# The token gate's dot product on VectorE, V in whole tiles, and a new order, in a hand-planned attention and feed-forward kernel

## The chip, the core and the metric

The kernel runs on one core of one Trainium2 chip. A core has five engines that run side by side: TensorE (PE, matrix products), VectorE (DVE), ScalarE (ACT), GpSimd (POOL) and SyncE (SP), which here only issues DMAs. Each engine takes its instructions strictly in the order in which the program lists them, and one that waits for a semaphore holds up all behind it. The metric is device time in microseconds (us), a median over runs.

## The reference

Two branches read the same `x` (2048 rows of 512, bf16) and are mixed by a gate for each row:

```python
x = A_x
g = _sigmoid((x * gate_w).sum(-1, keepdims=True))
a = _A_ref(x, A_wq, A_wk, A_wv, A_wo, A_beta)
b = _B_ref(x, B_W_gate, B_W_up, B_W_down)
return g * a + (1 - g) * b
```

`_B_ref` is a feed-forward block with 1792 hidden columns: `gate = x @ W_gate`, `up = x @ W_up`, `h = relu(gate) * up`, `h @ W_down`. `_A_ref` is attention with 32 heads of 16 columns in four segments of 512 rows. For each segment `s`:

```python
logits = einsum('bhqd,bhkd->bhqk', qs, ks) * scale + mask
a_dot = einsum('bhqk,bhkd->bhqd', softmax(logits), vs)
a_mem = einsum('bhld,bhde->bhle', phi(qs), M) / den
o = g * a_mem + (1.0 - g) * a_dot            # g = sigmoid(beta), per head
M = M + einsum('bhld,bhle->bhde', phi(ks), vs)   # likewise z, for den
```

with `phi(t) = t + 1 where t > 0, else exp(t)`; then `o @ wo`. The gate of a row is thus a dot product of that row of `x` with `gate_w`, and it is this dot product that the change moves.

## The kernel before

Every piece of work is a step of a planner. `add(name, engines, emit, after, prio, lat, take, give)` gives a step its possible engines with a cost on each, the steps it waits for, a due number (`prio`), the time `lat` until its result counts as there, and the PSUM banks that it takes or gives back. `lay_out` plays the plan through by these costs: whenever an engine comes free it takes, of the steps whose predecessors are done, the one with the lowest rank. The rank is `prio`, plus the entry of `SHIFT` for the step's kind, plus a tenth of the step's own entry in `NUDGE`, a list of 1090 numbers in the order in which steps are added. An engine that is free takes any step that is ready, however late its rank. The order that results is written out as the program. On the chip only the order stays, with semaphores; the costs and due times are the plan's alone.

PSUM holds four banks `rb` of 512 columns for all products but the attention scores, which have four banks of their own (`sp`).

The steps that matter here, by segment `seg`, column block `c` and row tile `t` of 128 rows:

- **Start.** `early` steps are DMAs issued at once on SP or ACT: the four row tiles of segment 0 (into `xn`, the same memory as `xT[1]`), then V's, K's and Q's weights. `E_G` stands for the load of `gate_w` and `beta` into `gin` by POOL, and counts as landed at 6.0. `XP` steps transpose the row tiles on PE, `XA` steps copy them to `xT[0]` on DVE or ACT. `YP`, `YD`, `YA`, `YH`, `YL` compute the heads' gates; `YP` also turns `gate_w` into a column, which `YD` copies into column 512 of `wv_sb`.
- **Weights of the feed-forward.** `wg0`..`wg3` and `wu0`..`wu3` are eight DMAs on SP, `wd` and `wo` the down and output weights. `wd` waits for the transposes of K's features in segment 0.
- **Projections.** `Q`, `K` (L491) and their copies `QC`, `KC`; `KO` masks K (L504, L506). V of segment 0 (L516) comes piece by piece as its weight lands. V of the later segments (L533) is done in two halves of 256 columns for each row tile, the second with column 512, the token gate, behind it: 257. `VC` copies a half (L389, L387), and the second half's also clamps the gate's column into `zg` (L543). For segment 0 `TP` (L579) is a product of its own for the column, `TG` (L587) its clamp.
- **Row gates.** `TE` (L593) takes the exponential of `zg`, `TN` (L598) and `TL` (L603, L606) go on from it.
- **Attention.** `QK` (L738) fills `sp`, `EX` (L749) is its exponential on ACT, `MK` (L759) the mask on POOL, `PV` (L808) the product with V, followed by a chain on DVE.
- **Memory.** `EK` (L626) takes the exponential of K into `e1k`, `MN` (L632) its minimum with 1, `PK` (L636) puts phi(K) into `pkT`, and `KX` is a DMA transpose of `pkT` into `pK`, issued on SP. `XT` steps are DMA transposes of segments 1 to 3 of `x`.
- **Feed-forward.** `G`, `U` (L918), `R` (L930, L932), `H` (L937), `D` (L952), `W` (L965), `OS`, and the store `ST` on SP.

Of the kernel before, what the change touches and what calls it, by code (L numbers as in the profile page):

```python
# [13 lines left out]
P = 128  # L14
# [24 lines left out]
SHIFT = {'PA': 15, 'PB': 0, 'LIKE': 35, 'T': -43, 'PQ': 42, 'N': -104, 'MZ': -228, 'PV': -136, 'OS': -150, 'OC': -94, 'R': -63, 'EX': -241, 'QK': -81, 'KC': 5, 'H': -95, 'KTR': -235, 'TG': -121, 'PK': -281, 'VC': -64, 'MN': 30, 'XC': 118, 'MK': 208, 'K': -25, 'U': 10, 'D': 11, 'EK': 57, 'MQ': 24, 'EQ': -42, 'TR': 201, 'MA': -36, 'KO': 124, 'V': -15, 'G': 8, 'QC': 201, 'KX': 50, 'W': 72, 'Q': -21, 'OX': 45, 'TA': -65, 'GS': 41, 'TL': -45, 'TN': 103, 'TB': 8, 'MR': 0}  # L39
# [181 lines left out]
def mm(n, k=1):  # L221
    return k * (n / 2400.0 + 0.0025)
# [806 lines left out]
```

## Time and profile before

| | |
|---|---|
| median of 3 runs | 269.93 us (269.28 to 272.64) |
| the profiled execution, its time | 270.74 us |
| its span in the profile | 269.0 us |
| clock granted to PE | 1.0 |
| DMA, read and written | 8.13 and 2.10 MB of device memory |

The page of the profile gives busy time and count of instructions of each engine, the chain of work that ended last, and the costliest groups. A timeline lists start and duration in us, the engine, the line in the kernel, the operation, `out<-in` with shapes, and a count; a bracket gives the idle time of the engine just before and what released it. PEld is PE's weight load, SPq the DMA queue of SP. Windows give busy us of each engine within stretches of the span:

```
0.00:5.00 5.00, 3.67 (x29) 2.98 (x30) 1.17 (x10) 2.23 (x4) 4.13 (x12) 1.00 0.58 166
5.00:10.00 5.00, 4.99 (x27) 2.17 (x25) 1.36 (x7) 2.77 (x7) 3.27 (x8) 1.00 0.94 291
10.00:16.00 6.00, 6.00 (x50) 2.78 (x48) 3.77 (x10) 4.30 (x8) 3.28 (x8) 1.00 1.09 369
16.00:24.00 8.00, 8.00 (x66) 3.33 (x66) 5.04 (x11) 7.03 (x6) 2.70 (x6) 1.00 1.09 260
24.00:36.00 12.00, 10.52 (x125) 5.20 (x131) 9.10 (x23) 10.10 (x13) 7.67 (x16) 1.00 0.93 150
36.00:80.00 44.00, 43.94 (x754) 20.30 (x751) 36.16 (x82) 37.46 (x35) 31.47 (x80) 1.00 0.24 59
80.00:130.00 50.00, 50.00 (x746) 22.26 (x745) 39.14 (x89) 39.90 (x36) 32.75 (x72) 1.00 0.12 29
```

The columns after the stretch and its length are PE, PEld, DVE, ACT and POOL with their instruction counts, the granted clock, the busy share of the DMA engines, and GB/s.

### The profile page before, as it was taken

To read this page: it belongs to the slowest core of one execution; us is meant where nothing else is said; L and a number is where in the kernel's file an instruction comes from. 1 tells how busy PE (TensorE), PEld (TensorE's weight loads), DVE (VectorE), ACT (ScalarE), POOL (GpSimd) and SP (SyncE) were. 2 spreads that over 40 slices of the span, in tenths; PEclk is the share of its full clock that TensorE was granted. 3 is DMA by queue.
4 is the path that set the end of the run, shared out by engine and by line. 5 is a ranking of instruction groups with operands and counts; after the bars stand their busy time and mean duration, and the time that the engine had idled before them with its cause. 6 is when DMAs were issued, how large, how long until landed. Compare 5 with 4: busy or idle time off the path is not lost.

```text
span 269.0 us, 8042 instructions
## 1 busy us (share of the span) xinstructions
PE 263.0 (98%) x3365; PEld 120.9 (45%) x3365; DVE 185.3 (69%) x414; ACT 192.3 (71%) x185; POOL 162.4 (60%) x378
## 2 busy tenths in 40 slices
PE   8999799999999999999999999999999999999995
PEld 5444344444455444444444544444444444344444
DVE  1477697799489966986767767897826535878800
ACT  3789799987689977777979777765659757876021
POOL 8435767465888874655684888645425685735400
PEclk9999999999999999999999999999999999999999
DMA  6997980420302310000030000000010100000011
GB/s 202 327 347 150 120 273 5 57 66 2 80 2 73 73 43 22 2 2 0 13 68 22 23 19 2 23 4 0 2 45 22 37 5 22 0 4 2 2 39 39
DMA packets 26293, 15.06 MB, mean 56 GB/s; under 512 B 13585, under 2 KB 26257, under 8 KB 26257
## 3 DMA queue, kind: packets, MB, share of 16 engines
q1 hardware_dynamic: 25904, 14.29, 21.1%
q8 instruction: 26, 0.43, 0.7%
q10 hardware_dynamic: 288, 0.26, 0.3%
q14 instruction: 11, 0.08, 0.1%
q0 software_dynamic: 64, 0.00, 0.0%
HBM read 8.13 MB, written 2.10 MB: 38 GB/s over the span
## 4 chain that ended last, share of the span: by engine, by line
PE 94%; DMA 3%; ACT 1%; SPq 1%; DVE 0%; issue 0%; DVEq 0%; ACTq 0%
PE rb L918 37%; PE rb L952 17%; PE rb L491 10%; PE sp L738 9%; PE rb L808 7%; PE rb L965 5%; PE rb L533 3%; DMA wu_sb<-in_B_W_up_dram 2%; PE rb L516 2%; PE rb L876 1%; PE rb L779 1%; DMA xT<-in_A_x_dram 1%; ACT E L749 1%; PE rb L650 1%; PE rb L404 1%; SPq L352 1%
## 5 line engine op out<-in xcount | busy, mean ns | idle before, releaser
L749 ACT ACTIVATE E<-sp 128x2048 bf16<-128x2048 f32 x72 | 135.1, 1876 | 36.2 <-PE sp L738 34.4
L759 POOL TENSOR_SCALAR_AFFINE_SELECT E<-E 64x256 bf16<-64x256 bf16 x256 | 112.9, 441 | 77.3 <-ACT E L749 65.1
L918 PE MATMUL rb<-xT,wu_sb 128*128 128x512 bf16 x224 | 55.9, 380 | 1.5 <-DMA wu_sb<-in_B_W_up_dram 1.5
L918 PE MATMUL rb<-xT,wg_sb 128*128 128x512 bf16 x224 | 55.6, 380 | 0.0
L937 DVE TENSOR_TENSOR hT<-rb,rg 128x512 bf16<-128x512 f32 x56 | 38.1, 683 | 24.7 <-PE rb L918 15.7
L952 PE MATMUL rb<-wd_sb,hT 128*128 128x512 bf16 x210 | 49.2, 380 | 0.0
L918 PEld LDWEIGHTS <-wu_sb 128*128 128x128 bf16 x224 | 20.5, 98 | 26.9 <-issue 3.0
L918 PEld LDWEIGHTS <-wg_sb 128*128 128x128 bf16 x224 | 20.3, 98 | 26.2 <-issue 4.3
L738 PE MATMUL sp<-QT,KT 16*64 16x320 bf16 (+7 forms) x512 | 30.3, 295 | 0.1
L952 PEld LDWEIGHTS <-hT 128*128 128x128 bf16 x210 | 19.3, 98 | 24.6 <-issue 3.5
L738 PE MATMUL sp<-QT,KTo 32*64 32x320 bf16 (+7 forms) x512 | 30.3, 295 | 0.0
L930 ACT ACTIVATE rg<-rb 128x512 bf16<-128x512 f32 x35 | 20.8, 595 | 8.8 <-PE rb L918 7.0
L826 DVE STREAM_TRANSPOSE tA<-rb 128x512 f32<-128x512 f32 x32 | 20.8, 689 | 7.0 <-PE rb L808 7.0
L738 PEld LDWEIGHTS <-KT 16*64 16x64 bf16 x512 | 10.6, 102 | 28.3 <-issue 28.3
L974 ACT ACTIVATE osb<-rb,ngcol 128x512 bf16<-128x512 f32 x11 | 7.5, 685 | 15.9 <-PE rb L965 15.9
L808 PE MATMUL rb<-E,Vs 64*32 64x448 bf16 (+7 forms) x512 | 18.8, 284 | 0.0
L808 PE MATMUL rb<-E,Vp 64*32 64x448 bf16 (+7 forms) x512 | 18.4, 284 | 0.0
L491 PE MATMUL rb<-xT,wq_sb 128*128 128x512 bf16 x64 | 16.3, 380 | 0.0
L491 PE MATMUL rb<-xT,wk_sb 128*128 128x512 bf16 x64 | 16.1, 379 | 0.0
L965 PE MATMUL rb<-wo_sb,oT 128*128 128x512 bf16 x60 | 15.1, 380 | 0.0
L932 DVE TENSOR_SCALAR rg<-rb 128x512 bf16<-128x512 f32 x21 | 14.2, 682 | 1.3 <-PE rb L918 0.7
L389 DVE CAST QT<-rb 128x512 bf16<-128x512 f32 x11 | 7.6, 687 | 9.4 <-PE rb L491 9.4
(107 smaller groups left out, 313.9 us busy)
## 6 DMA issues: line engine op xcount, KB each, us to landing
out_dram<-osb SPq DMA_DIRECT2D x15, 128.0 KB, 1.7
wd_sb<-in_B_W_down_dram SPq DMA_DIRECT2D x1, 1792.0 KB, 7.5
wg_sb<-in_B_W_gate_dram SPq DMA_DIRECT2D x3, 512.0 KB, 7.7
wu_sb<-in_B_W_up_dram SPq DMA_DIRECT2D x3, 512.0 KB, 7.8
Vs<-Vp SPq DMA_DIRECT2D x8, 144.0 KB, 3.4
wk_sb<-in_A_wk_dram SPq DMA_DIRECT2D x2, 256.0 KB, 4.5
wq_sb<-in_A_wq_dram SPq DMA_DIRECT2D x2, 256.0 KB, 5.5
wo_sb<-in_A_wo_dram SPq DMA_DIRECT2D x1, 512.0 KB, 6.8
```

Source lines behind the costliest of these rows:

```text
L491: nc.tensor.matmul(rb[s.bank][:], lhsT=w[:, ci, c * P:(c + 1) * P], rhs=xT[i][:, ci, :], start=(ci == 0), stop=(ci == NC - 1))
L738: nc.tensor.matmul(sp[64 * h:64 * h + 64, j, off:off + m], lhsT=kt[32 * j:hi, c0 + w, 64 * ck:64 * ck + 64], rhs=QT[i][32 * j:hi, c0 + w, ...
L749: nc.scalar.activation(Er[n % NE][:], sp[:], ACT.Exp, scale=SCALE)
L759: nc.gpsimd.affine_select(out=v, in_=v, compare_op=ALU.is_ge, fill=0.0, base=0, pattern=[[0, 4], [1, 64]], channel_multiplier=-1)
L808: nc.tensor.matmul(rb[s.banks[h]][32 * j:32 * j + 32, q0:q0 + m], lhsT=v[64 * h:64 * h + 64, ck // 2, o:o + 32], rhs=Er[(base + f) % NE][6 ...
L826: nc.vector.transpose(tA[k].rearrange("p b w -> p (b w)"), rb[a.banks[r]][:])
L918: nc.tensor.matmul(rb[s.bank][:], lhsT=w[:, ci, fv * P:(fv + 1) * P], rhs=xT[i][:, ci, :], start=(ci == 0), stop=(ci == NC - 1))
L930: nc.scalar.activation(rgb[k][:], rb[a.bank][:], ACT.Relu)
L932: nc.vector.tensor_scalar(rgb[k][:], rb[a.bank][:], 0.0, None, ALU.max)
L937: nc.vector.tensor_tensor(hT[:, fv, :], rb[a.bank][:], rgb[k][:], ALU.mult)
L952: nc.tensor.matmul(rb[b][:], lhsT=hT[:, fv, lc:lc + P], rhs=wd_sb[:, fv, :], start=(fv == 0), stop=False)
L965: nc.tensor.matmul(rb[hold.bank][:], lhsT=oT[i][:, ci, lc:lc + P], rhs=wo_sb[:, ci, :], start=False, stop=(ci == NC - 1))
```

## The change

- The row gate's dot product leaves PE. `gate_w` is loaded, repeated on all 128 partitions, into `gwb` by a DMA that POOL issues behind the memsets of `Vp` and `Vs`; `gin` holds only `beta`. For each row tile one DVE instruction (`TG`) multiplies the tile's rows by `gwb` and adds up along the row into `zg`; `TC` clamps the four columns of a segment. Segment 0 uses the rows in `xn`; for the later segments SP loads two row tiles at a time into `xg` (`XG`, 256 KB, six in all).
- The transpose `XT1` overwrites `xn`, so it now also waits for segment 0's four products; it is added later, in `project(1)`.
- V of segments 1 to 3 is one product of 512 columns and one copy for each row tile, and no longer waits for `YD`.
- V's weight: pieces 1 and 3 come on ACT's queue (only piece 1 did).
- `PK` writes over `e1k`, and `KX` reads it from there. `EK` of column `c` now waits for `KX` two columns earlier instead of `PK`.
- `wo` waits for the K transposes of segment 0, as `wd` does.
- The plan's times: a DMA's `lat` 3.5 instead of 2.0, a transpose's 2.8 and 2.2 instead of 2.4 and 1.6, some early landings. `E_G` keeps 6.0. `TG` joins `PORT`, the kinds that the plan takes to hold up POOL, and `TC` gets `TG`'s shift of -121.
- All of `NUDGE` is new, and so the order of everything.

```diff
-    nc.gpsimd.dma_start(out=gin[0:NC, 0:P], in_=gate_w.rearrange("(c p) -> c p", p=P))
-    nc.gpsimd.dma_start(out=gin[0:1, P:P + H], in_=A_beta.rearrange("(o h) -> o h", o=1))
+    nc.gpsimd.dma_start(out=gin[0:1, 0:H], in_=A_beta.rearrange("(o h) -> o h", o=1))
     for i in range(2):
         nc.gpsimd.memset(Vp[i][:], 1.0)
         nc.gpsimd.memset(Vs[i][:, :, VR:], 0.0)
 
+    nc.gpsimd.dma_start(out=gwb[:], in_=gate_w.rearrange("(o d) -> o d", o=1).to_broadcast([P, D]))
...
-    ld_x[1] = load_xT(1, xps, prio=6)
...
-            d["xT"] = [ld_x[1]]
+            d["xT"] = [load_xT(1, xps + st[0]["tg"], prio=6)]
...
+            def pv(e, s, t=t):
+                for ci in range(NC):
+                    nc.tensor.matmul(rb[s.bank][:], lhsT=xT[i][:, ci, t * P:(t + 1) * P],
+                                     rhs=wv_sb[:, ci, :], start=(ci == 0), stop=(ci == NC - 1))
...
+        for t in range(4):
+            if seg and t % 2 == 0:
+                rows_in = dma("SP", xg[:], rows(x[seg * L + t * P:seg * L + (t + 2) * P, :]),
+                              after=gates[-2:], prio=t_unit(seg, 0) - 30.0, kb=256, name=f"XG{seg}{t}")
+
+            def tok(e, s, t=t):
+                nc.vector.scalar_tensor_tensor(xg[:, t % 2, :], xg[:, t % 2, :] if seg else xn[:, t, :], 1.0, gwb[:],
+                                               ALU.mult, ALU.mult, accum_out=zg[:, seg * 4 + t:seg * 4 + t + 1])
+            d["zg"].append(add(f"TG{seg}{t}", {"DVE": 0.605}, tok,
+                               after=[rows_in if seg else xin[t], ld["gw"]] + (xps if seg == 1 else []),
+                               prio=t_unit(seg, 0) - 1.0))
...
-            b = add(f"EK{seg}{c}", {"ACT": act(L, True)}, ek, after=[d["K"][c]] + kph[-2:][:1] * (len(kph) > 1),
+            b = add(f"EK{seg}{c}", {"ACT": act(L, True)}, ek, after=[d["K"][c]] + kts[-2:][:1] * (len(kts) > 1),
...
-                nc.vector.scalar_tensor_tensor(pkT[c % 2][:], KT[i][:, c, :], 0.0, e1k[c % 2][:],
+                nc.vector.scalar_tensor_tensor(e1k[c % 2][:], KT[i][:, c, :], 0.0, e1k[c % 2][:],
...
-                ld["wd"].after += st[0]["PK"]
+                for w in ("wd", "wo"):
+                    ld[w].after += st[0]["PK"]
```

Entries of `NUDGE` that the prediction uses, found by counting steps in the order in which they are added:

| step | due number | entry before | entry after |
|---|---|---|---|
| wu1 (columns 256 to 767 of the up weight) | 3 | 2300 | 104 |
| wu3 (columns 1280 to 1791) | 5 | 47 | 258 |
| XT1 | 6 | 83 | 1084 |
| TG00, the first product | 18, shift -121 | none | -9020 |

More of the change, by code (lines that the diff above doesn't have):

```diff
@@ L35 @@
 NCH = 2
-SHIFT = {'PA': 15, 'PB': 0, 'LIKE': 35, 'T': -43, 'PQ': 42, 'N': -104, 'MZ': -228, 'PV': -136, 'OS': -150, 'OC': -94, 'R': -63, 'EX': -241, 'QK': -81, 'KC': 5, 'H': -95, 'KTR': -235, 'TG': -121, 'PK': -281, 'VC': -64, 'MN': 30, 'XC': 118, 'MK': 208, 'K': -25, 'U': 10, 'D': 11, 'EK': 57, 'MQ': 24, 'EQ': -42, 'TR': 201, 'MA': -36, 'KO': 124, 'V': -15, 'G': 8, 'QC': 201, 'KX': 50, 'W': 72, 'Q': -21, 'OX': 45, 'TA': -65, 'GS': 41, 'TL': -45, 'TN': 103, 'TB': 8, 'MR': 0}
+SHIFT = {'PA': 15, 'PB': 0, 'LIKE': 35, 'T': -43, 'PQ': 42, 'N': -104, 'MZ': -228, 'PV': -136, 'OS': -150, 'OC': -94, 'R': -63, 'EX': -241, 'QK': -81, 'KC': 5, 'H': -95, 'KTR': -235, 'TG': -121, 'TC': -121, 'PK': -281, 'VC': -64, 'MN': 30, 'XC': 118, 'MK': 208, 'K': -25, 'U': 10, 'D': 11, 'EK': 57, 'MQ': 24, 'EQ': -42, 'TR': 201, 'MA': -36, 'KO': 124, 'V': -15, 'G': 8, 'QC': 201, 'KX': 50, 'W': 72, 'Q': -21, 'OX': 45, 'TA': -65, 'GS': 41, 'TL': -45, 'TN': 103, 'TB': 8, 'MR': 0}
 KEEP = {'D': 2, 'U': 1, 'Q': 2, 'G': 1, 'V': 1, 'MZ': 1}
@@ L42 @@
 NUDGE = [
[56 rows of a table removed]
[55 rows of a table added]
 ]
 T0, TU, SPAN, PEN_D, PEN_A, PEN_P = 19.0, 15.6, 4.1, -23.0, 150.0, 146.0
-PORT = {'KO', 'MB', 'MQ', 'MN', 'GS', 'PQ', 'PK', 'N1', 'N2', 'N3', 'NM'}
+PORT = {'TG', 'KO', 'MB', 'MQ', 'MN', 'GS', 'PQ', 'PK', 'N1', 'N2', 'N3', 'NM'}
 PIECE = {'MK': 0.445, 'TL': 0.22, 'ZE': 0.24, 'YL': 0.22, 'MB': 0.3}
@@ L260 @@
     ones = sb([P], BF16, "ones")
-    gin = sb([P + H], BF16, "gin")
+    gin = sb([H], BF16, "gin")
+    gwb = sb([D], BF16, "gwb")
+    xg = sb([2, D], BF16, "xg")
     mcol_o = sb([1], F32, "mcol_o")
@@ L285 @@
     wk_sb = sb([NC, D], BF16, "wk_sb")
-    wv_sb = sb([NC, D + 2], BF16, "wv_sb")
+    wv_sb = sb([NC, D], BF16, "wv_sb")
     wo_sb = sb([NC, D], BF16, "wo_sb")
@@ L311 @@
     e1k = [sb([L], BF16, f"e1k{i}") for i in range(2)]
-    pkT = [sb([L], BF16, f"pkT{i}") for i in range(2)]
     rgb = [sb([L], BF16, f"rg{i}") for i in range(NRG)]
@@ L332, with dma @@
         nc.gpsimd.memset(Vs[i][:, :, VR:], 0.0)
+    nc.gpsimd.dma_start(out=gwb[:], in_=gate_w.rearrange("(o d) -> o d", o=1).to_broadcast([P, D]))
     plan = Plan(range(4))
     add = plan.add
-    def dma(eng, o, i, after=(), prio=0.0, kb=512, lat=2.0, name="dma"):
+    def dma(eng, o, i, after=(), prio=0.0, kb=512, lat=3.5, name="dma"):
         key = {"SP": nc.sync, "ACT": nc.scalar, "POOL": nc.gpsimd}[eng]
@@ L352, in transpose @@
                    lambda e, s: nc.sync.dma_start(out=o, in_=i, transpose=True),
-                   after=[e_q, *after], prio=prio, lat=2.4 if kb > 128 else 1.6)
+                   after=[e_q, *after], prio=prio, lat=2.8 if kb > 128 else 2.2)
     def load_xT(seg, after=(), prio=0.0):
@@ L364 @@
     xin = [early("SP", xn[:, 0, :], x[0:P, :], 3.35), early("ACT", xn[:, 1, :], x[P:2 * P, :], 3.55)]
-    ld["V"] = [early(("SP", "ACT", "SP", "SP")[ci], wv_sb[:, ci, 0:D], A_wv[ci * P:(ci + 1) * P, :],
-                     (4.0, 4.2, 5.1, 5.6)[ci]) for ci in range(NC)]
-    xin += [early("SP", xn[:, t, :], x[t * P:(t + 1) * P, :], 6.4 + 1.0 * (t - 2)) for t in (2, 3)]
-    ld["K"] = [early("SP", wk_sb[:, h:h + 2, :], rows(A_wk)[:, h:h + 2, :], 8.0 + 0.35 * h) for h in (0, 2)]
-    ld["Q"] = [early("SP", wq_sb[:, h:h + 2, :], rows(A_wq)[:, h:h + 2, :], 9.6 + 0.7 * h) for h in (0, 2)]
+    ld["V"] = [early(("SP", "ACT", "SP", "ACT")[ci], wv_sb[:, ci, :], A_wv[ci * P:(ci + 1) * P, :],
+                     (4.0, 4.2, 5.0, 5.3)[ci]) for ci in range(NC)]
+    xin += [early("SP", xn[:, t, :], x[t * P:(t + 1) * P, :], 6.0 + 0.5 * (t - 2)) for t in (2, 3)]
+    ld["K"] = [early("SP", wk_sb[:, h:h + 2, :], rows(A_wk)[:, h:h + 2, :], 7.2 + 0.7 * h) for h in (0, 2)]
+    ld["Q"] = [early("SP", wq_sb[:, h:h + 2, :], rows(A_wq)[:, h:h + 2, :], 9.3 + 0.4 * h) for h in (0, 2)]
     ld["gw"] = ld["beta"] = add("E_G", {"QEG": 0.01}, lambda e, s: None, prio=-2000.0, lat=6.0)
@@ L412 @@
             xtr[t].append(add(f"XA{t}{h}", {"DVE": dve(2 * P), "ACT": act(2 * P)}, xe, after=[a], prio=-900.0, give=a))
-    ld_x[1] = load_xT(1, xps, prio=6)
     eb, gbt, gb = (sb([H], F32, n) for n in ("eb", "gbt", "gb"))
     def gates_mm(e, s):
-        nc.tensor.matmul(rb[s.bank][:, 0:NC], lhsT=gin[:, 0:P], rhs=ident[:, 0:NC], start=True, stop=False,
-                         skip_group_check=True)
-        nc.tensor.matmul(rb[s.bank][:, 32:32 + H], lhsT=ones[:], rhs=gin[:, P:P + H], start=False, stop=True,
-                         skip_group_check=True)
-    gm = add("YP", {"PE": 0.06}, gates_mm, after=[ld["gw"], ld["beta"]], prio=9.0, take=True, lat=0.25)
+        nc.tensor.matmul(rb[s.bank][:, 0:H], lhsT=ones[:], rhs=gin[:], start=True, stop=True)
+    gm = add("YP", {"PE": 0.03}, gates_mm, after=[ld["gw"], ld["beta"]], prio=9.0, take=True, lat=0.25)
     def gates_out(e, s):
-        nc.vector.tensor_copy(wv_sb[:, :, D], rb[gm.bank][:, 0:NC])
-        nc.vector.tensor_scalar(betac[:], rb[gm.bank][:, 32:32 + H], 80.0, -80.0, ALU.min, ALU.max)
-    go = add("YD", {"DVE": 0.25}, gates_out, after=[gm], prio=9.0, give=gm)
+        nc.vector.tensor_scalar(betac[:], rb[gm.bank][:, 0:H], 80.0, -80.0, ALU.min, ALU.max)
+    go = add("YD", {"DVE": 0.14}, gates_out, after=[gm], prio=9.0, give=gm)
     def gates_exp(e, s):
@@ L469, in t_unit @@
         return T0 + TU * (NC * seg + c)
-    st = {}
+    st, gates = {}, []
     def project(seg):
@@ L516, in pv @@
                         nc.tensor.matmul(rb[(a or s).bank][:], lhsT=xT[i][:, ci, t * P:(t + 1) * P],
-                                         rhs=wv_sb[:, ci, 0:D], start=(ci == 0), stop=(ci == NC - 1))
+                                         rhs=wv_sb[:, ci, :], start=(ci == 0), stop=(ci == NC - 1))
                     last = add(f"VI{t}{ci}", {"PE": 0.4 if t < 2 and ci < 2 else mm(L)}, pv,
@@ L527, in project, with vc @@
                 continue
-            for h in range(2):
-                n = D // 2 + h
-                def pv(e, s, t=t, h=h, n=n):
-                    for ci in range(NC):
-                        nc.tensor.matmul(rb[s.bank][:, 0:n], lhsT=xT[i][:, ci, t * P:(t + 1) * P],
-                                         rhs=wv_sb[:, ci, h * D // 2:h * D // 2 + n], start=(ci == 0), stop=(ci == NC - 1))
-                a = add(f"V{seg}{t}{h}", {"PE": mm(n, NC)}, pv,
-                        after=d["xT"] + ld["V"] + [go] + (old["pv"] + old["mz"] if old else []),
-                        prio=want, take=True, lat=0.3)
-                d["xr"].append(a)
-                def vc(e, s, a=a, t=t, h=h):
-                    by_parity(e, Vh[i][:, t, :, 8 * h:8 * h + 8, 0:DH], rb[a.bank][:, 0:D // 2])
-                    if h:
-                        nc.vector.tensor_scalar(zg[:, seg * 4 + t:seg * 4 + t + 1], rb[a.bank][:, D // 2:D // 2 + 1],
-                                                80.0, -80.0, ALU.min, ALU.max)
-                v = evac(D // 2)
-                if h:
-                    v = {"DVE": (v["DVE"][0] + 0.09, PEN_D)}
-                d["V"].append(add(f"VC{seg}{t}{h}", v, vc, after=[a], prio=want, give=a))
-                if h:
-                    d["zg"].append(d["V"][-1])
+            def pv(e, s, t=t):
+                for ci in range(NC):
+                    nc.tensor.matmul(rb[s.bank][:], lhsT=xT[i][:, ci, t * P:(t + 1) * P],
+                                     rhs=wv_sb[:, ci, :], start=(ci == 0), stop=(ci == NC - 1))
+            a = add(f"V{seg}{t}", {"PE": mm(L, NC)}, pv,
+                    after=d["xT"] + ld["V"] + (old["pv"] + old["mz"] if old else []),
+                    prio=want, take=True, lat=0.3)
+            d["xr"].append(a)
+            def vc(e, s, a=a, t=t):
+                by_parity(e, Vh[i][:, t, :, :, 0:DH], rb[a.bank][:])
+            d["V"].append(add(f"VC{seg}{t}", evac(L), vc, after=[a], prio=want, give=a))
         shift_v(seg)
@@ L572, in project, with tokc @@
                                    after=[m] + (old["mr"] if old else []), prio=want))
-        if seg == 0:
-            def tokp(e, s):
-                for t in range(4):
-                    for ci in range(NC):
-                        nc.tensor.matmul(rb[s.bank][:, t:t + 1], lhsT=xT[i][:, ci, t * P:(t + 1) * P],
-                                         rhs=wv_sb[:, ci, D:D + 1], start=(t == 0 and ci == 0),
-                                         stop=(t == 3 and ci == NC - 1), skip_group_check=True)
-            p = add(f"TP{seg}", {"PE": 16 * 0.026}, tokp, after=d["xT"] + [go],
-                    prio=t_unit(seg, 0) - 1.0, take=True, lat=0.25)
-            d["xr"].append(p)
-            def tok(e, s, p=p):
-                nc.vector.tensor_scalar(zg[:, seg * 4:seg * 4 + 4], rb[p.bank][:, 0:4], 80.0, -80.0, ALU.min, ALU.max)
-            a = add(f"TG{seg}", {"DVE": 0.1}, tok, after=[p], prio=t_unit(seg, 0) - 1.0, give=p)
-            d["zg"] = [a]
+        d["zg"] = []
+        for t in range(4):
[8 more added lines that the diff above has]
+                               prio=t_unit(seg, 0) - 1.0))
+            gates.append(d["zg"][-1])
+        d["tg"] = d["zg"]
+        def tokc(e, s):
+            cols = slice(seg * 4, seg * 4 + 4)
+            nc.vector.tensor_scalar(zg[:, cols], zg[:, cols], 80.0, -80.0, ALU.min, ALU.max)
+        d["zg"] = [add(f"TC{seg}", {"DVE": 0.07}, tokc, after=d["zg"], prio=t_unit(seg, 0) - 1.0)]
         def tok2(e, s):
@@ L635, in pk @@
             def pk(e, s, c=c):
-                nc.vector.scalar_tensor_tensor(pkT[c % 2][:], KT[i][:, c, :], 0.0, e1k[c % 2][:],
+                nc.vector.scalar_tensor_tensor(e1k[c % 2][:], KT[i][:, c, :], 0.0, e1k[c % 2][:],
                                                ALU.max, ALU.add)
-            p = add(f"PK{seg}{c}", {"DVE": dve(L)}, pk, after=[m] + kts[-2:][:1] * (len(kts) > 1), prio=want)
-            kph.append(p)
+            p = add(f"PK{seg}{c}", {"DVE": dve(L)}, pk, after=[m], prio=want)
             d.setdefault("kr", []).append(p)
-            kts.append(transpose(f"KX{seg}{c}", pK[:, :, c * P:(c + 1) * P], pkT[c % 2][:],
+            kts.append(transpose(f"KX{seg}{c}", pK[:, :, c * P:(c + 1) * P], e1k[c % 2][:],
                                  [p] + prevmz, want, 128))
@@ L861, in attend @@
             otr.append(d["oT"][-1])
-    fills, readers, masks, kph, kts, otr, chains, pvs, mems, sums = [], {}, {}, [], [], [], [], [], [], []
+    fills, readers, masks, kts, otr, chains, pvs, mems, sums = [], {}, {}, [], [], [], [], [], []
     rgn, rgu, sts = [0], [], []
```

111 rows, old and new, of the table NUDGE are left out of this document.

## The prediction

> **What bounds the kernel now.** I read the page first, the row of busy times and the chain that ended last, and then the timeline of each engine.
>
> ```profile
> PE 263.0 (98%) x3365; PEld 120.9 (45%) x3365; DVE 185.3 (69%) x414; ACT 192.3 (71%) x185; POOL 162.4 (60%) x378
> PE 94%; DMA 3%; ACT 1%; SPq 1%; DVE 0%; issue 0%; DVEq 0%; ACTq 0%
> ```
>
> TensorE (PE) is the bound: 263.0 of 269.0 us. Its timeline shows where the other 6 us are; these are all the lines with idle time before them:
>
> ```profile
> 1.05 2.21 PE L394 MATMUL rb<-zeros 128*128 128x128 bf16 x19 [1.05 <-DVE zeros L265]
> 3.54 1.03 PE L404 MATMUL rb<-ident,xT 128*128 128x128 bf16 x8 [0.28 <-DMA xT<-in_A_x_dram]
> 31.53 1.04 PE L918 MATMUL rb<-xT,wu_sb 128*128 128x512 bf16 x4 [1.48 <-DMA wu_sb<-in_B_W_up_dram]
> ```
>
> 1.05 + 0.28 + 1.48 = 2.8 us, and some 3.1 us of tail after the last matmul. From 31.5 us on PE never waits. So a change can win only what it takes from PE's work, the 1.48 us, and a better start; whatever it makes PE wait for is lost in full. Pieces of PE work are priced from the chain in order of time:
>
> ```profile
> 4.58 2.44 PE rb L516 x6
> 11.76 0.38 PE rb L579 x16
> 48.48 0.86 PE rb L491 x4
> 50.21 0.44 PE rb L533 x4
> ```
>
> Four 512-column matmuls take 0.86 us, four of 256 or 257 take 0.44. The six early V matmuls take 0.407 us each, about twice the later 0.215.
>
> For the start I need GpSimd (POOL) and the DMA queue of SP:
>
> ```profile
> 1.98 0.76 POOL L328 DMA_DIRECT2D gin<-in_gate_w_dram  x1
> 2.74 0.53 POOL L329 DMA_DIRECT2D gin<-in_A_beta_dram  x1
> 3.27 2.09 POOL L331 MEMSET Vp<- 128x2368 bf16 x1
> 5.36 2.09 POOL L331 MEMSET Vp<- 128x2368 bf16 x1
> ```
>
> ```profile
> 14.08 7.10 SPq L352 DMA_TRANSPOSE xT<-in_A_x_dram  x1
> 21.30 1.36 SPq L464 DMA_DIRECT2D Vs<-Vp  x2
> 22.75 2.57 SPq L352 DMA_TRANSPOSE pK<-pkT  x2
> 25.38 0.58 SPq L340 DMA_DIRECT2D wu_sb<-in_B_W_up_dram  x1
> ```
>
> **The change, part by part** (plus is slower).
>
> *PE's work.* The token column's 16 matmuls go: -0.38. Per row tile V costs 2 x 0.44 = 0.88 now and 0.86 as one piece: 12 x 0.02 = -0.24. The transposed `gate_w` (one tiny matmul, 0.04 in the chain) is nothing. Sum **-0.6**, all on the path.
>
> *The wait of 1.48.* The last piece of `wu_sb` is issued at 25.38 because the transpose of segment 1's rows, the copies of V and two transposes of K stand ahead of it on SP. A step's rank is its due number plus a shift plus a tenth of its NUDGE entry. Before, that piece (wu1) has 3 + 230 = 233 and the transpose XT1 6 + 8.3 = 14.3; after, wu1 has 3 + 10.4 = 13.4, the last weight (wu3) 5 + 25.8 = 30.8 and XT1 6 + 108.4 = 114.4. All eight pieces now go first, at about 14 us, some 11 us earlier, and 512 KB of `wo_sb` (issued at 6.17) leave the stream, worth 1.4 to 2.0 us at the 260 to 369 GB/s that the windows show from 10 to 24 us. So **-1.48** (0 at worst). XT1 is then late: it landed 9.1 us after its issue, first needed at 25.05; issued near 15 us, behind the token products, it lands at about 24. I count 0; if that cover is gone, the wait is some 1 us, inside the order's bound below.
>
> *The gate weight.* The beta DMA stays first on POOL, the memsets follow, and `gwb` is issued behind them: 1.98 + 0.53 to 0.76 + 4.3 of memsets, about 6.9 us. The two small loads there landed 3.6 and 3.3 us after issue, which gives 10.3. But this one is 128 KB in the busiest stretch (DMA engines 94% busy at 5 to 10 us, full after): the 256 and 512 KB loads on SP took 4.5 to 7.8. So it lands between 10.2 and 14.7; I take 11, near the small loads, since it has a queue of its own. The Trainium skill, "DMA: Bandwidth & Descriptors", section "Anatomy of one DMA — SWDGE (gpsimd) path", fits a GpSimd DMA as 2.0 us plus bytes over 436 GB/s, which is 2.3 us for 128 KB and would land it at 9.2, with the sum some 1.8 us lower. The trace doesn't agree: 64 bytes took 3.3 us.
>
> The plan has not been told: E_G still says 6.0, which was right for the old loads (2.74 + 3.3 = 6.0). The first product TG00 has rank 18 - 121 - 902 = -1005, so VectorE (DVE) takes it at 6.0 in the plan, before anything else, and DVE's queue keeps that order on the chip. Behind it stand the other products, any share of the eight copies `XA` that falls to DVE, `YD`, `YH`, then KO and the copies of K. At present:
>
> ```profile
> 7.43 0.29 DVE L389 COPY xT<-rb 128x256 bf16<-128x256 bf16 x1
> 11.12 0.35 DVE L506 TENSOR_SCALAR KTo<-KT,mcol_o 128x512 bf16<-128x512 bf16 x1 [2.52 <-ACT KT L387]
> 11.39 0.68 DVE L389 CAST KT<-rb 128x512 bf16<-128x512 f32 x1
> ```
>
> If one `XA` copy stands behind TG00, K's first matmul moves from 9.44 to 11 + one or two products (0.61 each, the step between neighbouring DVE instructions) + 0.3 + 0.1 = 12 to 12.6. If ScalarE (ACT) has all of them, what is next are KO and K's copies, at 11 + 4 x 0.61 = 13.4 against 11.12, and `YA` on ACT, which waits for `YD` and holds ACT's copies behind it. Either way PE is 2.3 to 3.1 us short of work, less what it can draw ahead (V's last matmuls, 0.43). Bounds 0 (DVE is idle 2.2 of the 6 us from 10 and 3.0 of the 8 from 16) and 8.7 (14.7 - 6.0). I take **+2.3**.
>
> *DVE after the start.* 12 further products at 0.69 (the like instruction, L636, has a median of 693 ns) = 8.3, four clamps at 0.16 = 0.6; gone are 12 zg clamps at 0.147 = 1.8, and 24 copies of 0.41 become 12 of 0.69: -1.6. Net +5.5 spread over 150 us in which DVE is 78 to 82% busy (36.16 of 44, 39.14 of 50). It hides, except where a product stands ahead of a copy that frees a bank: 0.61 each. Bounds -0.5 (fewer, whole-bank copies) and +1.5; I take **+0.3**, near zero because PE shows no wait at that load today. An accumulating product may take longer than L636; no row here shows one.
>
> *K's features in place.* ACT's exponential EK of column c + 2 now waits for the transpose of c to land, no longer for a DVE step. The plan gives a transpose 1.25 + 2.2 = 3.45 us; rows: 2.3, 2.9, 5.9 from issue (lowest, median, highest), 3.7 in the first 30 us. Queued behind a waiting EK are ACT's score exponentials (L749, 135.1 us in all) and its copies from PSUM, and PE waits for those. Bounds 0 and 3 (the four of segment 0, up to 2.5 late each, ACT 84% busy there); I take **+0.5**, since DVE's own wait for these transposes is 0.7 today.
>
> *The rest costs nothing.* `wd_sb` is issued at 32.2 already and lands 7.5 later; `wo_sb` behind it lands near 42 and is first needed at 78. Six loads of 256 KB of token rows take SP 0.6 us each to issue in stretches with DMA 3 to 24% busy; a store or K transpose behind one is 0.6 late.
>
> *The order.* All 1090 NUDGE entries are new. Today's order leaves PE no gap after 31.5. Best, ten of the 0.11 us that a piece costs after a change of tile shape (0.97 against 0.86) are saved: -1; worst, gaps of +3; I take **+0.5**.
>
> **Sum:** -0.6 - 1.48 + 2.3 + 0.3 + 0.5 + 0.5 = +1.5. The profiled execution took 270.74, 1.7 outside its span, and lies 0.8 above the median; 270.74 + 1.5 = 272.2 for it, and 269.93 + 1.5 = **271.4** by the median.
>
> **Rivals.**
> 1. *The late gate weight is hidden* (0.22). ACT takes every `XA` copy, DVE catches up in its idle time. Then -0.6 - 1.5 + 0.3 + 0 to 0.8 = -1 to -1.8: 268.1 to 269. For it: DVE is idle for 2.27 us before 7.17 and for 2.52 before 11.12. Against: three of the last four copies were on ACT, not four.
> 2. *ACT's queue stands behind K's transposes* (0.25), the one that ends slower by over 2%. The mechanism decides once transposes land later than 3.45 us after their turn as a rule, because token-row loads, stores and X's transposes hold SP. Eight of 12 EKs late by 1.2 us (the spread from the median 2.9 to beyond 3.45, with one 0.6 issue ahead) cost 9 us on an ACT that is 75 to 84% busy; two thirds reach PE, 6: 269.93 - 2.1 + 2.3 + 6 = 276, up to 279. For it: SP transposes took 2.57 and 4.88 us a pair in segment 0. Against: only 0.7 us of waits on them now.
> 3. *PE goes cold* (0.08). The trace shows half speed for PE's first 6 us (0.407 a matmul until 7.0). If PE is idle long enough near 9 to 13 us to fall back, 3.4 to 6 us at half speed cost 1.7 to 3 more: 273.1 to 274.4. The Trainium skill, "TensorE: Matmul & The Clock Gate", section "Part 1: The HAM clock gate", lets the clock fall after an idle window of about 3.4 us. No gap in this trace is that long, so none shows it.
> 4. *Faster by over 2%* (0.02). It needs 5.4 us where 2.1 can be named.
>
> The forecast has the remaining 0.43. Two per cent (264.5 to 275.3) is about what a measurement of this kernel can tell from no change. Faster 0.02; slower 0.25 from rival 2 plus 0.05 from the gate weight's upper bound, 0.30; within 0.68. The range takes in rival 1 and most of rival 2, 268.0 to 278; the forecast's own is 269.5 to 273.5.
>
> **What would show it.** Right: an idle DVE until 10 to 12 us ahead of the first product, released by the load of `gwb`; a PE gap between 8 and 16 us released by DVE or ACT; no wait for `wu_sb` near 30; no L579. Rival 2: ACT idle ahead of L626 with a DMA named, and PE gaps from 24 us on. Wrong altogether: `gwb` landed by 7 us, or PE gaps late in the kernel that no part above names.

## The result and the profile after

The changed kernel takes 280.81 us (median; 280.46 to 281.42) against 270.0: a ratio of 1.0384, 95% interval 1.0312 to 1.0457. It is slower by 10.8 us, outside the range of the prediction. The profiled execution took 281.42 with a span of 279.7, 10.7 more than before.

The page of the changed kernel, busy times and the chain that ended last:

```profile
PE 266.6 (95%) x3300; PEld 117.6 (42%) x3300; DVE 189.5 (68%) x415; ACT 193.9 (69%) x189; POOL 168.3 (60%) x383
PE 73%; POOL 18%; DVE 3%; issue 3%; DMA 2%; ACT 0%; POOLq 0%; DVEq 0%
```

PE is no longer alone on the chain. Its timeline shows the large gap, and what the 12 matmuls behind it cost:

```profile
9.86 1.02 PE L487 MATMUL rb<-xT,wk_sb 128*128 128x512 bf16 x4
16.26 5.02 PE L487 MATMUL rb<-xT,wk_sb 128*128 128x512 bf16 x12 [5.38 <-ACT Vp L388]
21.11 1.03 PE L487 MATMUL rb<-xT,wq_sb 128*128 128x512 bf16 x4
```

PE is idle for 5.38 us, until ACT's copy of V (L388) frees a bank. Then 12 matmuls take 5.02 us, 0.42 each, where 12 x 0.215 = 2.58 is the time at the rate of the prediction's chain (0.86 for four): 2.44 us more. The window over this stretch has a granted clock of 0.51 (the third number from the end):

```profile
14.00:21.00 7.00, 4.74 (x12) 1.67 (x12) 4.89 (x18) 3.50 (x8) 2.09 (x11) 0.51 0.36 86
```

The wait for `wu_sb` near 30 us is gone, as forecast. Why ACT was late is seen on the other queues, in the timelines of POOL, DVE and ACT:

```profile
4.80 2.10 POOL L330 MEMSET Vp<- 128x2368 bf16 x1
6.81 0.18 POOL L331 MEMSET Vs<- 128x64 bf16 x1
6.90 0.58 POOL L333 DMA_DIRECT2D gwb<-in_gate_w_dram  x1
```

```profile
4.06 0.72 DVE L390 COPY xT<-rb 128x256 bf16<-128x256 bf16 x2 [2.50 <-PE rb L405]
12.52 0.69 DVE L567 SCALAR_TENSOR_TENSOR xg<-xT,gwb 128x512 bf16<-128x512 bf16 x1 [7.74 <-DMA gwb<-in_gate_w_dram]
...
15.21 0.08 DVE L567 DVE_READ_ACCUMULATOR xg<-xT,gwb 128x1 f32 x1
15.33 0.17 DVE L578 TENSOR_SCALAR zg<-zg 128x4 f32<-128x4 f32 x1
```

```profile
8.83 0.41 ACT L388 COPY xT<-rb 128x256 bf16<-128x256 bf16 x1
15.53 0.20 ACT L583 ACTIVATE rcol<-zg 128x4 f32<-128x4 f32 x1 [6.30 <-DVE zg L578]
15.64 1.05 ACT L388 CAST Vp<-rb 128x512 bf16<-128x512 f32 x2
16.59 0.24 ACT L426 ACTIVATE eb<-betac 128x32 f32<-128x32 f32 x1
```

The load is issued at 6.90 and lands at 12.5. DVE stands still for it for 7.74 us, does four products and the clamp, and only then ACT, which has been waiting for that clamp for 6.30 us with the exponential of the row gate (`TE0`), gets to the two copies of V behind it. By the order of the steps PE's four banks are then held by these two, by K's first block, and by `YP`, which `YD` on DVE has yet to read.

The wait goes on to a third queue. SP's DMAs that copy V (`Vs<-Vp`) wait for ACT's copies, and the feed-forward weights stand behind them:

```profile
6.06 0.92 SPq L341 DMA_DIRECT2D wg_sb<-in_B_W_gate_dram  x2
16.78 0.70 SPq L460 DMA_DIRECT2D Vs<-Vp  x1
...
20.61 2.21 SPq L341 DMA_DIRECT2D wu_sb<-in_B_W_up_dram  x2
```

A second loss is later, and small gaps only hint at it: from 60 to 110 us PE has seven, of 0.2 to 0.7 us and 2.4 in all, five of them ended by DVE and one by POOL. It is easier to see against the plan. The score exponentials on ACT come in the same order in every kernel, 72 of them; the table gives how late the n-th one starts against the time that the kernel's own plan has for it (us; the plan of the changed kernel, and for the first and the last column that of the kernel before).

| n | before | after | e1 | e4 | e5 | e6 | e7 | e8 | e9 |
|---|---|---|---|---|---|---|---|---|---|
| 0 | 0.3 | 8.1 | 4.2 | 2.6 | 2.2 | 2.4 | 2.3 | 0.0 | 0.1 |
| 3 | 0.2 | 8.3 | 4.3 | 2.4 | 3.6 | 2.2 | 3.8 | 0.1 | 0.1 |
| 9 | 1.9 | 8.2 | 5.1 | 2.4 | 3.5 | 2.1 | 3.6 | 0.6 | 0.1 |
| 15 | 2.0 | 8.4 | 5.3 | 2.6 | 3.7 | 1.9 | 3.4 | 0.4 | 0.2 |
| 21 | 1.7 | 9.6 | 6.6 | 3.8 | 6.1 | 1.8 | 3.5 | 0.3 | -0.1 |
| 27 | 1.9 | 10.9 | 7.9 | 5.1 | 7.3 | 2.7 | 4.0 | 1.1 | 0.1 |
| 48 | 1.8 | 10.9 | 7.9 | 5.0 | 7.1 | 2.7 | 4.0 | 1.1 | 0.0 |
| 71 | 2.1 | 11.1 | 8.2 | 5.3 | 7.3 | 3.0 | 4.2 | 1.4 | 0.3 |

Before, the chip followed its plan to within 0.3 us, lost the wait for `wu_sb` (1.7) and nothing more. The changed kernel is 8.1 late at the first scores, loses 2.5 more between the 15th and the 27th (61 to 98 us of the plan, 69 to 109 on the chip), and then holds. Besides, its plan is longer: the last step starts at 266.3 in it, against 264.8 before.

### The profile page after: what moved, and what is told of

Same layout as the page of the kernel before. It is cut to its first block, busy times and chain, and to the rows that moved or that the text cites. A ratio compares the mean times of both kernels' runs of the same rounds, so it can differ in the third digit from the quotient of the medians.

```text
span 279.7 us, 7933 instructions
## 1 busy us (share of the span) xinstructions
PE 266.6 (95%) x3300; PEld 117.6 (42%) x3300; DVE 189.5 (68%) x415; ACT 193.9 (69%) x189; POOL 168.3 (60%) x383
## 4 chain that ended last, share of the span: by engine, by line
PE 73%; POOL 18%; DVE 3%; issue 3%; DMA 2%; ACT 0%; POOLq 0%; DVEq 0%
PE rb L907 31%; PE rb L941 13%; POOL E L748 10%; PE rb L487 8%; PE sp L727 7%; PE rb L797 5%; PE rb L954 4%; PE rb L526 3%; DMA gwb<-in_gate_w_dram 2%; POOL mnum L657 2%; POOL coefM L700 2%; POOL Vp L330 1%; PE rb L865 1%; POOL e1k L622 1%; DVE xg L567 1%
## 5 line engine op out<-in xcount | busy, mean ns | idle before, releaser
L748 POOL TENSOR_SCALAR_AFFINE_SELECT E<-E 64x256 bf16<-64x256 bf16 x256 | 118.6, 463 | 70.2 <-ACT E L738 57.5
L727 PEld LDWEIGHTS <-KT 16*64 16x64 bf16 x512 | 10.9, 103 | 29.6 <-issue 29.5
L487 PE MATMUL rb<-xT,wk_sb 128*128 128x512 bf16 x64 | 18.1, 422 | 5.4 <-ACT Vp L388 5.4
L963 ACT ACTIVATE osb<-rb,ngcol 128x512 bf16<-128x512 f32 x12 | 8.2, 687 | 18.4 <-PE rb L954 16.7
L797 PE MATMUL rb<-E,Vs 64*32 64x448 bf16 (+7 forms) x512 | 19.6, 284 | 0.2
L700 POOL COPY coefM<-dinv 32x32 f32<-32x32 f32 x48 | 12.1, 251 | 2.1
```

The lines of the kernel that those rows point to most:

```text
L487: nc.tensor.matmul(rb[s.bank][:], lhsT=w[:, ci, c * P:(c + 1) * P], rhs=xT[i][:, ci, :], start=(ci == 0), stop=(ci == NC - 1))
L700: nc.gpsimd.tensor_copy(coefM[i][32 * j:32 * j + 32].rearrange("p c (t q) r -> p c t q r", q=4)[:, :, :, q, :], dinv[32 * q:32 * q + 32].r ...
L727: nc.tensor.matmul(sp[64 * h:64 * h + 64, j, off:off + m], lhsT=kt[32 * j:hi, c0 + w, 64 * ck:64 * ck + 64], rhs=QT[i][32 * j:hi, c0 + w, ...
L748: nc.gpsimd.affine_select(out=v, in_=v, compare_op=ALU.is_ge, fill=0.0, base=0, pattern=[[0, 4], [1, 64]], channel_multiplier=-1)
L797: nc.tensor.matmul(rb[s.banks[h]][32 * j:32 * j + 32, q0:q0 + m], lhsT=v[64 * h:64 * h + 64, ck // 2, o:o + 32], rhs=Er[(base + f) % NE][6 ...
```

## The experiments

The theories: **A**, the late gate weight is the whole loss and what follows is an echo; **B**, the new order loses time of its own between 40 and 105 us; **C**, ACT's queue stands behind K's transposes (the prediction's rival 2).

**e1: the gate weight's load first.**

```diff
+    nc.gpsimd.dma_start(out=gwb[:], in_=gate_w.rearrange("(o d) -> o d", o=1).to_broadcast([P, D]))
     nc.gpsimd.dma_start(out=gin[0:1, 0:H], in_=A_beta.rearrange("(o h) -> o h", o=1))
...
-    nc.gpsimd.dma_start(out=gwb[:], in_=gate_w.rearrange("(o d) -> o d", o=1).to_broadcast([P, D]))
```

> The changed kernel with one line moved: POOL issues the load of the repeated gate weight as its first DMA, ahead of beta and the memsets, about 4.9 us earlier; the order of everything else is as it was. Theory A (the late gate weight is the whole loss): the first product starts near 7.5 instead of 12.5, the wait of 5.4 us before K's second block and the half-speed K matmuls (2.4 us) are gone, and later gaps, which only follow from that lag, go too: 269 to 271. Theory B (the new order also puts more work on POOL, whose chain from 52 to 102 us holds PE): the start is mended but gaps between 40 and 105 us stay, about 3 us: 273 to 275. Theory C (K's exponentials stand on ACT's queue behind K's transposes): little gain, 278 or more.

277.99 us, ratio to before 1.0291 (1.0214 to 1.0367). The timelines of DVE and PE in e1:

```profile
8.39 0.69 DVE L566 SCALAR_TENSOR_TENSOR xg<-xT,gwb 128x512 bf16<-128x512 bf16 x1 [3.44 <-DMA gwb<-in_gate_w_dram]
```

```profile
7.56 1.44 PE L511 MATMUL rb<-wv_sb,xT 128*128 128x512 bf16 x3 [1.65 <-DMA wv_sb<-in_A_wv_dram]
```

The first product starts at 8.39, later than forecast, and the gap of 5.38 is gone. But PE now waits 1.65 us for a piece of V's weight, which was there at 5.90 in the changed kernel, and its early matmuls stay slow for longer (V's 16 have a mean of 605 ns in the groups, against 471). That the extra 128 KB held up V's weight is the likely reason; no run separates it. Half of the start's loss is mended (4.2 late in place of 8.1), and the loss from the 15th to the 27th stays (5.3 to 7.9). Theory A as a whole falls. The time is the one that theory C named (278 or more), but not by its mechanism: in all of e1, ACT waits 1.1 us for K's transposes.

**e2: PE kept busy in the gap.**

```diff
+        if s.name == "K03":
+            for k in range(24):
+                nc.tensor.matmul(sp[:, 0, :], lhsT=zeros[:], rhs=xT[0][:, 0, :], start=True, stop=True)
         s.emit(s.start[2], s)
```

> The changed kernel with 24 products of zeros, 128x512 each (5.2 us at full speed), put on PE ahead of K's second block, where PE waits 5.4 us for a bank; they write to the score banks, which nobody uses yet. The wait stays, PE only stays busy in it. Theory A with the clock: K's 12 matmuls run at 0.215 us instead of 0.41, PE is some 2.4 us earlier from 19 us on, and the kernel takes 278 to 279. If the half speed comes from something other than the idle time: no change, 280.8. If POOL's chain from 52 us on is the bound by itself (theory B): the 2.4 us are won at 21 us and lost again by 102: 280 to 281.

279.68 us, 1.1 less than the changed kernel (ratio to before 1.0354, 1.0296 to 1.0412). PE's timeline:

```profile
16.26 2.75 PE L487 MATMUL rb<-xT,wk_sb 128*128 128x512 bf16 x12 [0.63 <-ACT Vp L388]
```

The bank comes at the same 16.26, and the 12 matmuls take 2.75 in place of 5.02: the half speed came from the idle time. The first scores are 2.27 us earlier, yet only 1.1 of it reaches the end by the medians, 1.6 by the last exponential of the two profiled executions (9.5 late in place of 11.1): PE then waits for `wu_sb` (0.31 at 29) and twice for a score exponential (0.72 at 38, 0.52 at 41). The expectation of 278 to 279 was a little too good.

**e3: the gates' steps behind K's fourth block.** `TE0, TN0, TL0, YD, YA, YH, YL` are written out behind `KC03`. The bank that `YD` reads has another product in it by then, so the heads' gates come from other numbers; the amount of work is the same.

> The changed kernel, with the steps that use the row gate and the head gates (TE0, TN0, TL0, YD, YA, YH, YL) written out behind KC03 instead of ahead of V's last two copies; the load of the gate weight stays late (12.5). ACT then has nothing that waits for DVE ahead of V's and K's first copies. If ACT's queue behind TE0 is what held PE's banks: V's copies run at 10 to 11 us, K's second block starts near 11 instead of 16.3, PE then waits only for DVE's KO and KC03 behind the products (some 2 to 3 us), stays warm or nearly so, and the kernel takes 275 to 278. If DVE's late products by themselves hold PE: the gap stays near 5 us and the time near 280.

278.19 us (1.0305, 1.0241 to 1.0369). PE's timeline:

```profile
9.32 3.61 PE L487 MATMUL rb<-xT,wk_sb 128*128 128x512 bf16 x16
12.77 1.03 PE L487 MATMUL rb<-xT,wq_sb 128*128 128x512 bf16 x4
17.67 3.57 PE L907 MATMUL rb<-xT,wg_sb 128*128 128x512 bf16 x8 [3.87 <-DVE KT L390]
```

With ACT free, K's 16 and Q's first four matmuls run at once and at full speed. Then PE waits 3.87 us for DVE's copy of K, and eight matmuls take 3.57 (0.45 each): the half speed has moved along. So both queues held PE, ACT's first and DVE's right behind it.

**e4: segment 0's products off both queues.** From here on the edit is a list of steps that are written out elsewhere (`GS0` multiplies the row gates and the heads' gates of segment 0):

```diff
+    moves = [("PK00", ["TG00", "TG02", "TG03", "TG01", "TC0", "TE0", "TN0", "TL0"]), ("H0_3", ["GS0"])]
```

> The changed kernel, the late load left as it is, with segment 0's four products and what follows from them (TG00 to TG03, TC0, TE0, TN0, TL0) written out behind PK00 on DVE, and GS0 behind H0_3: nothing that V's and K's first blocks need stands behind the gate weight, neither on DVE nor on ACT. If the start's loss is only that queue order: no PE gap between 10 and 17 us, K at full speed, first scores near 15.6 as before the change, and 273 to 275, the rest being the gaps from 40 to 102 us (theory B). If all later gaps are an echo of the start: 268 to 270. If the start is held by something else too (the feed-forward weights behind the copies of V on SP): a new gap near 15 to 20 us and 275 to 277.

275.51 us (1.0197, 1.0163 to 1.0231), 5.3 less than the changed kernel with the load as late as ever. The gap and the slow K are gone; what is left at the start is a wait of 1.84 us at 18 for ACT's copy of Q, which stands behind the moved gate step. The loss from the 15th to the 27th is untouched, 2.6 to 5.1: it is no echo of the start.

**e5: POOL's extra steps on DVE.** On e4; `MN` and `MB` steps that the new plan gives to POOL run on DVE.

> As e4_start_order, and POOL's minimum steps of K's features and its memory steps (MN01, MN03, MN10, MN12, MN13, MB0, MB1; 7.4 + 5 us on POOL) run on DVE in the same places of the order. If POOL's load from the new choice of engines is what holds PE from 50 to 102 us: 2 to 4 us less than e4. If DVE (96 to 99% busy from 70 to 90) is as tight: no change, or slower.

277.13 us (1.0253, 1.0216 to 1.0289), slower than e4 by 1.6. POOL's busy time falls from 167.9 to 156.5 us, and PE still waits. The changed kernel's chain ran through POOL for 18% of the span, but POOL was not the bound by itself: 11 us less of its work wins nothing. DVE is as full, as the windows of e5 and e4 show (PE, PEld, DVE, ACT and POOL behind the stretch and its length):

```profile
70.00:80.00 10.00, 8.31 (x145) 3.70 (x144) 9.96 (x27) 8.91 (x8) 8.77 (x16) 1.00 0.09 28
```

```profile
70.00:80.00 10.00, 9.38 (x148) 4.08 (x147) 9.97 (x27) 8.81 (x10) 9.12 (x19) 1.00 0.10 28
```

DVE is busy for 9.96 and 9.97 of these 10 us. With the added steps it holds PE for 1.55 us at 79, and the next window of e5 is at a lower granted clock, 0.83:

```profile
79.13 0.54 PE L676 MATMUL rb<-mden,pqT 128*128 128x8 bf16 x16 [1.55 <-DVE tA L815]
```

```profile
80.00:90.00 10.00, 9.78 (x73) 3.68 (x73) 8.99 (x24) 7.76 (x11) 8.49 (x31) 0.83 0.12 29
```

How much slower e5 is than e4 is not a clean number, since the granted clock was lower in all four of its executions (0.986 to 0.993) and in one of e4's; 1.2 us of the loss are at the start, a stretch that the last section tells of. But e5's fastest, 276.33, less these 1.2 us, is an estimate of 275.1, level with e4's 275.22 to 275.62 and not 2 to 4 us less.

**e6: the products of segments 2 and 3 later.** On e4; the loads of token rows, products, clamps and gate steps of segments 2 and 3 are spread over 105 to 200 us of the plan, short of their first use.

> As e4_start_order, and the token-row loads, products, clamps and what follows of segments 2 and 3, which the new order puts at 36 to 82 us of its plan, are spread over 105 to 140 and 150 to 200 us, short of their first use, where DVE is 70 to 78% busy. If these eight products ahead of their need crowd DVE and POOL in 40 to 102 us: 1.5 to 4 us less than e4. If they hide there as the prediction had it: no change against e4.

273.22 us (1.0116, 1.0084 to 1.0149), 2.3 less than e4. From the 15th to the 27th exponential 0.8 us are lost, not 2.5. The same window:

```profile
70.00:80.00 10.00, 9.81 (x166) 4.51 (x168) 9.01 (x22) 9.57 (x10) 8.14 (x20) 1.00 0.02 3
```

DVE has a tenth free, POOL nearly two, and PE works 9.81 of 10 us. (Some matmul records are missing in e4 to e7, so PE's busy time in them is a little low.)

**e7: the 12 later products left out**, with their loads.

> As e4_start_order, without the 12 products and six token-row loads of segments 1 to 3; the row gate's sums of these segments are zeros. It bounds what the products on DVE cost after the start: the prediction's step gave 0.3 (-0.5 to 1.5), so e4 less 0 to 1.5. If the products crowd DVE and POOL: e4 less 3 or more, and at least as fast as e6.

273.86 us (1.0130, 1.0099 to 1.0160), 1.65 less than e4 and not faster than e6. The table tells why: from the 15th to the 27th it loses 0.6, near e6's 0.8, but by the 3rd it is 1.6 later than e6, which the last section comes to. Its two executions at a granted clock of 1.0 took 273.31 and 273.39, against 273.02 to 273.22 for e6's three. e7 leaves the clamps and gate steps of these segments where they were, so it is the products and their loads that crowd; whether DVE's time or the hold on POOL that the plan reckons with (`PORT`) does it, no run separates. So e6's place for the products costs next to nothing, and the place in the new order cost some 2 us (e4's 2.5 less 0.6).

**e8: segment 0's products spread further back**, on e6:

```diff
+    moves = [("R0_0", ["TG00", "TG02"]), ("PK01", ["TG03"]), ("QC01", ["TG01"]), ("H0_1", ["TC0"]),
+             ("EX001", ["TE0"]), ("QC03", ["TN0", "TL0"]), ("H0_3", ["GS0"]), ...]
```

> As e6_products_late, with segment 0's products and what follows spread further back, behind the first R, PK01, QC01, H and the second score exponential, so that nothing of the first scores' copies (KC01, QC00) stands behind them; e4 and e6 still had a wait of 1.84 us there and their first scores 2.6 to 2.8 us late. Against its own plan e6 is 2.4 us late at the first scores and 2.95 at the last. If both losses are nothing but places in DVE's and ACT's queues: late by 0.3 to 0.8 at the last scores, so 270.5 to 271.3, which leaves the plan's own 1.5 us and takes off the wait of 1.48 that the kernel before has. If XT1, which waits for these products, now comes too late for segment 1: a new PE gap near 27 to 32 us and 272 or more.

272.01 us (1.0069, 1.0037 to 1.0100). The first scores are on the plan's time to 0.1 us; 0.6 and 0.7 us are then lost by the 9th and between the 15th and 27th, in PE gaps of 0.2 to 0.5 us that wait for score exponentials and for DVE. It misses its 270.5 to 271.3 by 0.7. The late load was left at 6.9 us throughout: it costs nothing where nobody stands behind it.

**e9: the kernel before, with one DMA moved.**

```diff
+    order = [s for s in plan.order if s is not ld["wu1"]]
+    at = next(n for n, s in enumerate(order) if s.name == "XT1")
+    order.insert(at, ld["wu1"])
```

> The kernel before, with one DMA moved: the piece of the up weight that PE waits for at 30 us (wu1) is issued on SP directly ahead of XT1 instead of behind it, the copies of V and two K transposes. By the prediction's step the wait of 1.48 us goes and nothing comes in its place: 268.2 to 268.8. If XT1 is then late for segment 1's V at 25 us by more than that: no change or slower.

268.96 us (268.3 to 269.32), ratio to before 0.9944 (0.9915 to 0.9973): 1.5 us less by the ratio (0.7 to 2.3), 1.1 by the medians, and 0.9 against the median of those executions of the kernel before whose granted clock was at least 0.998. The median lies 0.2 above the forecast. SP's queue in e9:

```profile
12.57 2.46 SPq L340 DMA_DIRECT2D wu_sb<-in_B_W_up_dram  x2
15.15 7.69 SPq L352 DMA_TRANSPOSE xT<-in_A_x_dram  x1
22.95 1.36 SPq L464 DMA_DIRECT2D Vs<-Vp  x2
```

PE has no gap between 3.4 us and its last matmul, and follows its plan to within 0.3 us to the end. This is the fastest of all, and it has none of the change but the place of that one load.

## Why the prediction was wrong

What the runs give for the 10.7 us of span, by the table's last row: 1.5 for the longer plan, 8.1 - 0.3 for the start, and 11.1 - 8.1 = 3.0 after it, against 1.8 after it before (the wait for `wu_sb` among them). That is 1.5 + 7.8 + 1.2 = 10.5.

- *PE's work, -0.6.* L579 is gone and V's pieces are whole. The saving is inside the plan's difference and no run shows it apart.
- *The wait of 1.48.* Right in its size: the gap is gone, and e9 wins 0.9 to 1.5 us by that move alone. But in the changed kernel it is gone partly by luck. The pieces were not issued at about 14 us ahead of everything: six of them stood behind the copies of V, and the last two went out from 20.61 us on, some 4 us before the 25.38 of the kernel before and not 11. They were in time because PE itself was 8 us late; in e2, where PE is 2.3 us earlier, the wait is back with 0.31 us. In e8, where V is copied on time, the same two are issued from 14.26 on and PE doesn't wait for them.
- *The gate weight, +2.3.* This is the step that failed, by its size; the mechanism was right. The load landed at 12.5, not 11, 5.6 us after its issue and inside the bounds. All `XA` copies that came later had fallen to ACT, the step's second case. From there it asked when DVE would be ready, and took off what PE could draw ahead. It named `YA` as what holds ACT, not `TE0`, which stood ahead of V's last two copies: PE ran out of banks at 10.9 and waited 5.38. And the half speed was put into a rival of its own (0.08) that would need an idle time of PE, while the forecast itself brought one: e2 measures its price as 2.27 us at the first scores. Together 5.38 + 2.44 = 7.8 in place of 2.3. The step's upper bound, 8.7, held this. What was missing is a wait that passes from one in-order queue to the next, which no later idle time of DVE takes back.
- *DVE after the start, +0.3.* Wrong: e6 wins 2.3 us by moving eight products. The step spread the 12 products over 150 us. But the shift of -121, meant for segment 0, makes every product urgent, and the plan takes them soon after their rows are there: the last ones at 72 us, where their gate is first needed at 210. That could be read from the due numbers in the diff. In the changed kernel's windows DVE is busy for 9.97 of 10 us from 70 to 80 and again from 80 to 90.
- *K's features in place, +0.5, and rival 2.* Not seen. In the whole changed kernel ACT waits 0.5 us for a K transpose, where DVE's 0.7 are gone. The rival's 276 to 279 came nearer to the time than the forecast did, for a reason that doesn't hold.
- *The order, +0.5.* The plan itself is 1.5 us longer with 0.6 us less work for PE, so the order looks worse by some 2 us as planned, within the bound of 3. The two plans also reckon with different landing times of DMAs, and no run separates these from the order.
- *Rivals 1 and 3.* The first had its condition, every later `XA` copy on ACT, but not what was to follow: PE ran out of banks before DVE could catch up. Its outcome is what e8 made by hand, with 272.0 and not 268 to 269, because of the longer plan and what is lost after the start. The third happened, as a part of the forecast's own mechanism. (Rival 2 puts ACT at 75 to 84% busy; the windows of the kernel before give 72 to 88%, which changes nothing here.)

On the half speed the Trainium skill, "TensorE: Matmul & The Clock Gate", section "Part 1: The HAM clock gate", has PE's clock halved after an idle window of about 3.4 us and restored after as long a busy one. The changed kernel agrees on the fall, after its gap of 5.38 us; its half speed lasts some 5 us, longer than that window. The gap of 1.84 us in e5 and e7 does not agree, see the last section.

## What to carry to other kernels

A moved load is priced by when the first engine that waits for it gets to it, and then by following every in-order queue behind that engine, until PE has no free bank; an idle time found in this way has to be charged with the slow clock that can follow it as well. Where a planner sets the order, its table of landing times is a part of the change: one due time was left at 6.0 for a load that lands at 12.5, and the order built on it cost more than all the rest. (e8 moves the steps by hand; no run gives the plan the true time.) Work that hides by its share of the busy time hides only if it is placed where that engine has time; urgent ranks copied from a step that is needed early pull it forward into the fullest stretch.

## What the runs showed of the hardware that was not expected

A gap of 1.84 us on PE before the first scores, of the same length in the profiled executions of e4, e5, e6 and e7, halved the speed of the matmuls soon after it in two of them. In e7 it is this one:

```profile
17.68 0.37 PE L731 MATMUL sp<-QT,KT 16*64 16x512 bf16 x1 [1.84 <-ACT QT L389]
```

PE's timelines of e6 and e7, the same seven matmuls behind it:

```profile
18.95 1.67 PE L907 MATMUL rb<-xT,wu_sb 128*128 128x512 bf16 x7
```

```profile
18.90 2.93 PE L911 MATMUL rb<-xT,wu_sb 128*128 128x512 bf16 x7
```

1.3 us are lost in e7 and e5 and none in e4 and e6, with gaps that begin within half a microsecond of each other. From 14 to 24 us the granted clock is 0.83 in e5 and e7 and 1.00 in e4 and e6. So a gap of a third of the changed kernel's is enough at times.

It is the execution that decides, and not the kernel, as the mean granted clock of the executions shows, wherever it is on record. It is either 0.998 and above, or 0.994 and below:

| longest wait of PE after the first 8 us, in the profiled execution | kernels | executions at 0.994 or below |
|---|---|---|
| 5.38 us | after | 4 of 4 |
| 3.87 | e3 | 3 of 4 |
| 1.84 | e4, e5, e6, e7 | 8 of 16 |
| 1.48 | before | 6 of 38 |
| 0.7 or less | e2, e8, e9 | 0 of 26 |

Within e7 the two at 0.992 and 0.994 took 274.38 and 274.32 us and the two at 1.0 took 273.31 and 273.39; e6's one at 0.994 took 274.50, its three at 1.0 took 273.02 to 273.22. In these rows a longer wait goes with a larger share at the lower clock; e5, with all of its four, has a second wait, the 1.55 us at 79. What decides in a single execution is left open. Where it fell is known for the profiled executions alone. The granted clock does not show the half speed of the first microseconds (the row says 1.00 there), so e1, whose wait of 1.65 us lies in them, is left out of the table.

An accumulating product on DVE is followed by a read of the accumulator of 0.08 us (L567 above): with it the four products of segment 0 start 0.62 to 0.73 us apart.
